# Loads of v on SyncE's queue instead of ScalarE's, and a last tile in two halves: windowed attention and an MLP mixer on one Trainium2 core

## The chip, the cores and the metric

The kernel runs on one core of a Trainium2 chip. The metric is the device time of one execution in microseconds: the median of the runs shown. The profile is one further execution, recorded by the hardware profiler; its times count from the span's start, the first instruction.

## The reference

Eight batches, eight heads, 576 positions, head size 64. Attention is allowed within 32 positions, and to and from 8 global positions given in `global_idx`. A token mixer and a channel mixer follow, each with a residual.

```python
scores = scale * np.matmul(q, k.transpose(0, 1, 3, 2))      # mask: |i-j| <= 32, or i or j global
attn = softmax(np.where(mask, scores, -1e9))
x = np.matmul(attn, v).transpose(0, 2, 1, 3).reshape(8, 576, 512)
h = np.maximum(x.transpose(0, 2, 1) @ w_tok1, 0) @ w_tok2   # 576 -> 256 -> 576
u = x + h.transpose(0, 2, 1)
out = u + np.maximum(u @ w_ch1, 0) @ w_ch2                  # 512 -> 1536 -> 512
```

Inputs and output are float32; the kernel computes in float16 with float32 sums.

## The kernel before, in words

Each batch goes through the same steps, and two batches are in flight.

- **Loads** (`loads`, L922): q and k in two pieces of four heads (`lq`, `lk`, L504), their last 64 rows (`lr`, L514), and v in five row chunks (`lv`, L523). Each of these tiles exists once, so a load of the next batch waits for the casts of this one. Batches 0 to 2 are loaded by SP and POOL; batches 3 to 7 have q and k on SP's queue and v on ACT's (L946).
- **Casts** to float16: `qk` (L534), `rn` (L531), `vsh` (L546). `vod` is `vsh` moved by 64 rows (L554).
- **Transposes** of q and k: by PE for batches 0 to 2, by DMA transposes on SP's queue for batches 3 to 7 (`rawr` L639, `raw` L643: one and eight for a batch), which DVE copies into `qT` and `kT` (L646 to L654).
- **Scores and values**: PE's scores (L673), ACT's exponential `e` (L683), DVE's mask (L689) and a copy for the global sums (`eg`, L692); global queries and keys in `lf`, `rf`; values (L740, L753), divided by DVE into `x` (L781).
- **Token mixer**: L803, relu `a` L812, L821, and `u` = x + h (L834; the last 64 rows of two batches share one tile `ul`, L837). `u` is transposed into `uT` by PE (L848, L850) or DMA (L853), `ul` into `uTl` (L843).
- **Channel mixer**: 12 groups of L866 (`chan1`) with relu `b` (L858 on ACT or L860 on DVE), L878 for the tile of `ul` (`b1l`), then L895 (`chan2`) for four row tiles of a batch and, once for two batches, the last tile of `ul`. DVE adds `u` to the bank and writes `osb` (L903, three buffers in turn), which is stored (L906 by POOL, by SP in the last batch; L909 for the last tile, 64 rows to each batch).

Nothing of the order is written out. Each step is recorded with `op`: its engine choices with an estimated cost, a priority, what it reads and writes, the PSUM bank it needs, and for a DMA an estimated work, packet count and delay. `run` (L119) is a list scheduler that runs while the program is built: it picks, engine by engine, what could start first by those estimates, and so fixes each engine's order and which of the eight PSUM banks a matmul group uses. On the chip each engine runs its list strictly in that order, and waits at a step whose input isn't there. So a changed estimate for a DMA moves compute on other engines.

The calls of the loads of batches 3 to 7, with the estimated issue times in the brackets, in us:

```python
            load_rest(b, pl, [("S", 0.65)])
            ...
                    load_qk(b, ti, slice(h, h + 4), pl + 1 + h / 2, [("S", 0.5)])
            load_v(b, pl + 6, [("A", 0.6)])
```

Of the kernel before, what the change touches and what calls it, by code (L numbers as in the profile page):

```python
# [8 lines left out]
F32 = mybir.dt.float32  # L9
# [6 lines left out]
P = 128  # L16
# [11 lines left out]
def kernel(  # L28
# [12 lines left out]
    nc = tc.nc  # L41
    B, H, S, D = q.shape
# [5 lines left out]
    NJ = DCH // P  # L48
    assert S == 576 and D == 64 and DM == 512 and DTOK == 256 and DCH == 1536
    LAST = S - P * (NT - 1)  # L50
# [27 lines left out]
    uls = [const.tile([P, DM], F16, name=f"ul{i}") for i in range(2)]  # L78
# [3 lines left out]
    b1l = const.tile([P, NJ, P], F16, name="b1l")  # L82
    osbs = [const.tile([P, DM], F32, name=f"osb{i}") for i in range(3)]
# [35 lines left out]
    def run(free, look, hop, warm_until):  # L119
# [41 lines left out]
        def drain(t):  # L161
            if t > clock[0]:
                flow(rings, clock[0], t)
                clock[0] = t
# [28 lines left out]
        while ready:  # L193
            cand = {}
            for i in ready:
                o = ops[i]
                t0, sl = 0.0, None
                if o["new"]:
                    sl = slot(o["new"][0], len(o["new"][1]), max([free["P"]] + list(at[i].values())))
                    if sl is None:  # L200
                        continue
                    t0 = max(t0, max(x[0] for x in sl))
                best = None
                for k, (e, c) in enumerate(o["opts"]):
                    st = max([free[e], t0] + [f + (hop if x != e else 0.0) for x, f in at[i].items()])
                    if o["dma"]:
                        ln, z = lanes["G" if e == "G" else "S"], filled["A" if e == "K" else e]
                        if len(ln) >= 8:
                            st = max(st, max(ln[-8], ln[-7], ln[-6]) + 2.5 if e == "A" else ln[-8])
                        room, x = RING - o["dma"][3], len(z)  # L210
                        while x and room >= z[x - 1][1]:
                            room -= z[x - 1][1]
                            x -= 1
                        if x:
                            st = max(st, z[x - 1][0])
                    if e == "P" and o["mode"] != mode:
                        c = c + 0.095
                    key = (st + c + 0.25 * k, e, st, c)
                    if best is None or key < best:
                        best = key  # L220
                cand.setdefault(best[1], []).append((best[2], o["pri"], i, best[3], sl))
            assert cand, ("stuck", banks, [(ops[i]["opts"], ops[i]["pri"], ops[i]["new"] and ops[i]["new"][1]) for i in ready])
            pick = None
            for e, cs in cand.items():
                lim = min(x[0] for x in cs) + look[e]
                x = min((x for x in cs if x[0] <= lim), key=lambda x: (x[1], x[0], x[2]))
                if pick is None or x[0] < pick[1][0]:
                    pick = (e, x)
            e, (st, _, i, c, sl) = pick
            o = ops[i]  # L230
            if e == "P":
                gap, spare = st - free["P"], [k for k in range(8) if (banks[k][1] is None or not open_uses[banks[k][1]]) and banks[k][0] <= free["P"]]
                if st < warm_until and gap > 0.52 and spare:
                    warm(min(spare, key=lambda k: (banks[k][0], k)), int((gap - 0.3) / (0.22 if st < 12.0 else 0.12)))
                mode = o["mode"]
            if o["new"]:
                kind, keys, shape, dt = o["new"]
                for key, (_, k) in zip(keys, sl):
                    home[key] = [k, k + 1] if kind == "S" else [k]
                    for z in home[key]:  # L240
                        banks[z] = (0.0, key)
                    ps_tile[key] = view(k, shape, dt)
            o["fn"](e)
            free[e] = st + c
            f = st + c + LAT[e]
            if o["dma"]:
                work, size, lag, packets = o["dma"]
                q = "A" if e == "K" else e
                drain(min(f, min(free[x] for x in "GSA")))
                f = land(q, f, work, size, i)  # L250
                filled[q].append((f, packets))
                f += lag
                lanes["G" if e == "G" else "S"].append(f)
                f += o["late"] + (LATE if st > 36.0 else 0.3)
            fin[i] = f
            log.append((st, f, e, i, max(o["deps"], key=lambda x: fin[x]) if o["deps"] else None))
            ready.discard(i)
            for key in o["ps"]:
                open_uses[key] -= 1
                for z in home[key]:  # L260
                    banks[z] = (max(banks[z][0], f + hop), key)
            for u in users[i]:
                left[u] -= 1
                if i in ops[u]["behind"]:
                    at[u][e] = max(at[u].get(e, 0.0), st + c)
                else:
                    x = "D" if o["dma"] else e
                    at[u][x] = max(at[u].get(x, 0.0), f)
                if not left[u]:
                    ready.add(u)  # L270
# [614 lines left out]
    nout = [0]  # L885

    def chan2(b, tau, pri):
        i, key = b % 2, ("o", b, tau)
        last = tau == NT - 1
        js = [range(0, 4), range(4, 8), range(8, 12)] if b == 0 else [range(0, 6), range(6, 12)]  # L890
        for part, jr in enumerate(js):
            def f(e, jr=jr):
                for j in jr:
                    w = b1l[:, j, :] if last else b1[:, j, P * tau : P * tau + P]
                    nc.tensor.matmul(ps_tile[key], lhsT=w, rhs=wc2[:, j, :], start=(j == 0), stop=(j == NJ - 1))  # L895
            r = [("wc2", t) for t in sorted({j // 4 for j in jr})]
            r += [("b1l", t) for t in range(3)] if last else [("b1", j) for j in range(NJ)]
            op([("P", 0.2165 * len(jr))], pri - 0.5 * part if b else pri + 5 * part, f, r=r, ps=[key], new=("M", [key], [P, 512], F32) if part == 0 else None)
        o = nout[0] % 3
        nout[0] += 1  # L900
        osb = osbs[o]
        def g(e):
            nc.vector.tensor_add(out=osb, in0=uls[b // 2 % 2] if last else u16s[i][:, tau], in1=ps_tile[key])  # L903
        op([("V", 0.62)], pri - 8, g, r=[("ul", b // 2 % 2, 0), ("ul", b // 2 % 2, 1)] if last else [("u", i, tau)], ps=[key], w=[("osb", o)])
        if not last:
            op([("G", 0.56) if b < B - 1 else ("S", 0.45)], pri + 5, lambda e: ENG[e].dma_start(out=out[b, P * tau : P * tau + P, :], in_=osb), r=[("osb", o)], dma=STORE)  # L906
        else:
            for z in range(2):
                op([("S", 0.45)], pri + 5, lambda e, z=z: nc.sync.dma_start(  # L909
                    out=out[b - 1 + z, S - LAST : S, :], in_=osb[64 * z : 64 * z + 64]), r=[("osb", o)], dma=(0.39, 2048, 0.8, 64))  # L910
# [11 lines left out]
    def loads(b, n0=0):  # L922
        pl = 100.0 * b - 145 if b != 1 else -174.0
        if b == 0:
            load_rest(0, -196, [("S", 0.65)])
            for hs in (slice(0, 2), slice(2, 4), slice(4, 8)):
                for ti in range(2):
                    load_qk(0, ti, hs, -195 + hs.start, [("S", 0.6)])
            load_v(0, -180, [("S", 0.6)])
            gate(-178, [("lv", NT - 4)], [lv[:, NT - 4, 0, 0:1]])  # L930
            return
        if b < PEB:
            if b == 1:
                pl = -173.9
            load_rest(b, pl, [("G", 0.73)], [n0] if b == 1 else ())
            for h in range(0, H, 4):
                for ti in range(2):
                    load_qk(b, ti, slice(h, h + 4), pl + 1 + h / 2 if b > 1 else pl + 0.1 + h / 100, [("G", 0.88)], [n0] if b == 1 else ())
            if b > 1:
                load_v(b, pl + 6, [("G", 0.87)])  # L940
        else:
            load_rest(b, pl, [("S", 0.65)])
            for h in range(0, H, 4):
                for ti in range(2):
                    load_qk(b, ti, slice(h, h + 4), pl + 1 + h / 2, [("S", 0.5)])
            load_v(b, pl + 6, [("A", 0.6)])  # L946

    def casts(b):
        pc = 100.0 * b - 140
# [109 lines left out]
```

## Time and profile before

| what | value |
|---|---|
| median of 3 runs | 314.24 us (314.05 to 315.2) |
| the profiled execution's own time | 314.6 us |
| its span, first to last instruction | 312.9 us, 7276 instructions |
| TensorE clock granted, mean | 0.987 |
| HBM read, written | 36.11 MB, 9.44 MB |
| transfers: SP's queue (q1), POOL's (q0), ACT's (q10) | 26.49, 18.45, 5.90 MB |

How to read it: PE is the matmul engine, PEld its weight loads, DVE VectorE, ACT ScalarE, POOL GpSimd, SP SyncE, which only issues transfers; SPq and ACTq rows are issues by those engines. A row of a timeline gives start and duration in us, engine, line, operation, output and inputs with shapes, and in brackets how long the engine was idle just before and what ended that. Lines such as L903 are those of the kernel before.

### The profile page before, as it was taken

How to read it: one execution, taken by the hardware profiler on the slowest of the kernel's cores; microseconds unless marked ns; L12 is line 12 of the kernel's file. 1: busy time of each engine (PE TensorE's matmuls, PEld its weight loads, DVE VectorE, ACT ScalarE, POOL GpSimd, SP SyncE). 2: the span in 40 equal slices, each digit the busy share in tenths (PEclk: the TensorE clock that was granted, in tenths of full speed). 3: DMA queues.
4: the chain of work that ended last, by engine and by line, in shares of the span. 5: the costliest groups of instructions: out<-in, count | busy, mean ns of one | idle time of the engine just before them, and what ended most of it. 6: DMA issues, size and time to landing. Idle time of an engine off the chain costs nothing.

```text
span 312.9 us, 7276 instructions
## 1 busy us (share of the span) xinstructions
PE 292.0 (93%) x2943; PEld 154.4 (49%) x2943; DVE 186.8 (60%) x410; ACT 180.5 (58%) x325; POOL 60.5 (19%) x109
## 2 busy tenths in 40 slices
PE   6979889997999979988999998999999999999994
PEld 4755545454474434533456444544555445444641
DVE  7789667569686674876675846964543357230021
ACT  4864895377987758841989376733742083305500
POOL 8589635632001100002000110002000200020000
PEclk9989999999999979999999999999999999999998
DMA  6989999999999999999979999924003211051013
GB/s 183 255 129 287 208 222 222 287 243 234 214 212 220 194 267 318 118 190 221 325 114 176 203 313 189 159 50 136 36 0 63 89 53 37 12 140 69 2 67 102
DMA packets 94660, 51.31 MB, mean 164 GB/s; under 512 B 73698, under 2 KB 89954, under 8 KB 94626
## 3 DMA queue, kind: packets, MB, share of 16 engines
q1 hardware_dynamic: 62480, 26.49, 40.3%
q0 software_dynamic: 8704, 18.45, 24.0%
q10 hardware_dynamic: 23442, 5.90, 11.1%
q8 instruction: 23, 0.38, 0.5%
q14 instruction: 11, 0.09, 0.1%
HBM read 36.11 MB, written 9.44 MB: 146 GB/s over the span
## 4 chain that ended last, share of the span: by engine, by line
PE 58%; DMA 26%; ACT 5%; DVE 5%; issue 2%; SPq 2%; POOL 1%; POOLq 0%; ACTq 0%; DVEq 0%
PE bank L895 22%; PE bank L866 21%; DMA lv<-in_v_dram 8%; DMA raw<-qk 6%; DMA lq<-in_q_dram 5%; PE bank L821 4%; DMA g_q<-in_q_dram,idx_i 3%; PE bank L673 3%; PE bank L803 2%; DMA lk<-in_k_dram 2%; PE bank L878 2%; ACT qk L534 2%; ACT vsh L546 2%; DVE osb L903 2%; PE bank L753 1%
## 5 line engine op out<-in xcount | busy, mean ns | idle before, releaser
L866 PE MATMUL bank<-uT,wc 128*128 128x512 f16 x384 | 94.0, 384 | 6.4 <-DVE osb L903 2.3
L895 PE MATMUL bank<-wc,b 128*128 128x512 f16 x384 | 88.3, 379 | 2.9 <-DVE osb L903 2.2
L858 ACT ACTIVATE b<-bank 128x512 f16<-128x512 f32 x88 | 52.5, 617 | 38.3 <-PE bank L866 38.3
L683 ACT ACTIVATE e<-bank 128x648 f16<-128x648 f32 x64 | 42.7, 737 | 30.0 <-PE bank L673 29.8
L895 PEld LDWEIGHTS <-b 128*128 128x128 f16 x384 | 36.7, 98 | 45.9 <-issue 4.2
L866 PEld LDWEIGHTS <-wc 128*128 128x128 f16 x384 | 35.2, 98 | 48.5 <-issue 8.7
L906 POOL DMA_DIRECT2D out_dram<-osb x28 | 16.1, 574 | 203.1 <-DVE osb L903 203.0
L903 DVE TENSOR_TENSOR osb<-u,bank 128x512 f32<-128x512 f16 x32 | 21.9, 686 | 45.3 <-PE bank L895 41.5
L546 ACT CAST vsh<-lv 128x512 f16<-128x512 f32 (+3 forms) x44 | 26.5, 620 | 9.7 <-DMA uT<-u 5.3
L689 DVE TENSOR_TENSOR e<-e,masku 128x1296 f16<-128x1296 f16 x28 | 23.3, 831 | 13.7 <-ACT e L683 13.2
L834 DVE TENSOR_TENSOR u<-x,bank 128x512 f16<-128x512 f16 x30 | 18.7, 681 | 15.0 <-PE bank L821 14.8
L781 DVE TENSOR_TENSOR x<-bank,rr 128x512 f16<-128x512 f32 x32 | 22.1, 691 | 1.1
L821 PE MATMUL bank<-a,w 128*128 128x512 f16 x80 | 20.1, 379 | 0.5 <-DVE a L809 0.3
L534 ACT CAST qk<-lq 128x512 f16<-128x512 f32 x26 | 16.2, 626 | 4.5 <-DMA lq<-in_q_dram 2.0
L803 PE MATMUL bank<-x,w 128*128 128x512 f16 x64 | 18.7, 379 | 0.0
L673 PEld LDWEIGHTS <-kT 64*128 64x128 f16 x576 | 11.2, 97 | 14.4 <-issue 13.6
L534 ACT CAST qk<-lk 128x512 f16<-128x512 f32 x27 | 16.9, 631 | 1.8 <-DMA lk<-in_k_dram 1.8
L654 DVE COPY qT<-raw 128x512 f16<-128x512 f16 x20 | 12.0, 602 | 7.2 <-DMA raw<-qk 7.1
L753 PEld LDWEIGHTS <-e 128*64 128x64 f16 x576 | 16.1, 116 | 0.1
L740 PE MATMUL bank<-rf,lf 128*64 128x264 f16 x144 | 15.6, 293 | 0.5 <-DVE rf L726 0.5
L753 PE MATMUL bank<-vsh,e 128*64 128x66 f16 x320 | 16.0, 199 | 0.0
L673 PE MATMUL bank<-qT,kT 64*128 64x72 f16 x576 | 15.4, 198 | 0.0
(164 smaller groups left out, 333.6 us busy)
## 6 DMA issues: line engine op xcount, KB each, us to landing
out_dram<-osb POOLq DMA_DIRECT2D x28, 256.0 KB, 4.3
lq<-in_q_dram SPq DMA_DIRECT2D x11, 512.0 KB, 6.4
lk<-in_k_dram SPq DMA_DIRECT2D x11, 512.0 KB, 7.9
lv<-in_v_dram ACTq DMA_DIRECT2D x15, 256.0 KB, 4.6
wc<-in_moe_w_ch_dram POOLq DMA_DIRECT2D x6, 512.0 KB, 12.8
lq<-in_q_dram POOLq DMA_DIRECT2D x4, 512.0 KB, 6.4
lk<-in_k_dram POOLq DMA_DIRECT2D x4, 512.0 KB, 11.0
lv<-in_v_dram ACTq DMA_DIRECT2D x10, 192.0 KB, 3.8
```

Of the source, the lines that this page charges most:

```text
L534: COPY[e](out=qk[:, ti, p].rearrange("q i (r d) -> q r i d", r=2), in_=(lq, lk)[ti][:, hs])
L546: COPY[e](out=vsh[i][a:z, c, :, 0:D], in_=lv[a:z, c])
L673: nc.tensor.matmul(ps_tile[keys[z]][:, u // 3, UW * (u % 3) : UW * (u % 3) + UW], lhsT=kT[r, 64 * u : 64 * u + P], rhs=qT[r, u // 2, UW * ...
L683: op([("A", 0.595)], pri + 1, lambda e, par=par: nc.scalar.activation(out=es[i][:, 2 * p + par].rearrange("p (n u) x -> p n u x", n=3), in ...
L689: op([("V", 0.85)], pri + 2, lambda e: nc.vector.tensor_mul(out=e2, in0=e2, in1=masku.unsqueeze(1).to_broadcast([P, 2, NB, UW])), r=["mask ...
L753: nc.tensor.matmul(o[:, VW * hh : VW * hh + VW], lhsT=es[i][:, h, 2 * tau + c, x : x + 64], rhs=vod[i][:, tau, h, :] if c else vsh[i][:, t ...
L803: nc.tensor.matmul(ps_tile[key][:, tt], lhsT=w, rhs=x16s[i][:, ch, :], start=(ch == 0), stop=(ch == NT - 1))
L821: nc.tensor.matmul(ps_tile[key], lhsT=w2[:, ch, P * tau - sh : P * tau - sh + P], rhs=a1[:, ch, :], start=(ch == 0), stop=(ch == 1 and not ...
L858: nc.scalar.activation(out=out, in_=in_, func=AF.Relu)
L866: nc.tensor.matmul(ps_tile[key], lhsT=wc1[:, cc, P * j : P * j + P], rhs=uT[:, cc, :], start=(cc == 0), stop=(cc == 3))
L895: nc.tensor.matmul(ps_tile[key], lhsT=w, rhs=wc2[:, j, :], start=(j == 0), stop=(j == NJ - 1))
L903: nc.vector.tensor_add(out=osb, in0=uls[b // 2 % 2] if last else u16s[i][:, tau], in1=ps_tile[key])
```

## The change

Three edits. The v loads of batches 3 to 7 are issued by SP, with an estimated 1.0 us each, and the estimate for an issue of a q or k load of these batches goes from 0.5 to 1.15 us. The scheduler also holds SP back when ACT issues a transfer, by 0.9 us per 1024 packets; with v gone from ACT, only the new stores at the end are such transfers. And the last tile of the last batch (64 rows each of batches 6 and 7) is computed as two halves of 256 columns, each with its own bank and its own addition, and each stored by two transfers, one on SP's queue and one on ACT's. Since the estimates changed, the scheduler orders SP, ACT, DVE and PE anew from batch 3's loads on. POOL's order is the same.

```diff
             if o["dma"]:
                 work, size, lag, packets = o["dma"]
                 q = "A" if e == "K" else e
+                if e == "A":
+                    free["S"] = max(free["S"], st) + 0.9 * o["dma"][3] / 1024
                 drain(min(f, min(free[x] for x in "GSA")))
...
     def chan2(b, tau, pri):
         i, key = b % 2, ("o", b, tau)
         last = tau == NT - 1
+        if last and b == B - 1:
+            osb = osbs[nout[0] % 3]
+            for z in range(2):
+                cs, kz = slice(256 * z, 256 * z + 256), ("o", b, tau, z)
+                def f(e, cs=cs, kz=kz):
+                    for j in range(NJ):
+                        nc.tensor.matmul(ps_tile[kz], lhsT=b1l[:, j, :], rhs=wc2[:, j, cs], start=(j == 0), stop=(j == NJ - 1))
+                op([("P", 1.31)], pri + z, f, r=[("wc2", t) for t in range(3)] + [("b1l", t) for t in range(3)], ps=[kz], new=("M", [kz], [P, 256], F32))
+                op([("V", 0.4)], pri - 8, lambda e, cs=cs, kz=kz: nc.vector.tensor_add(out=osb[:, cs], in0=uls[b // 2 % 2][:, cs], in1=ps_tile[kz]),
+                   r=[("ul", b // 2 % 2, 0), ("ul", b // 2 % 2, 1)] + ([] if z else [("osb", nout[0] % 3)]), ps=[kz], w=[("osbz", z)])
+                for y in range(2):
+                    op([("SA"[y], 0.45)], pri + 5 + z, lambda e, y=y, cs=cs: ENG[e].dma_start(
+                        out=out[b - 1 + y, S - LAST : S, cs], in_=osb[64 * y : 64 * y + 64, cs]), r=[("osbz", z)], dma=(0.25, 1024, 0.8, 64))
+            return
...
-                    load_qk(b, ti, slice(h, h + 4), pl + 1 + h / 2, [("S", 0.5)])
-            load_v(b, pl + 6, [("A", 0.6)])
+                    load_qk(b, ti, slice(h, h + 4), pl + 1 + h / 2, [("S", 1.15)])
+            load_v(b, pl + 6, [("S", 1.0)])
```

SP's order around the loads of batch 4 shows the move: `raw` and `rawr` are the transposes of batch 3, then of batch 4. Before:

```order
L643 DMA_TRANSPOSE raw<-qk 128x4x128 x3
L504 DMA lq<-in_q_dram 128x4x256
L504 DMA lk<-in_k_dram 128x4x256
L643 DMA_TRANSPOSE raw<-qk 128x4x128 x4
L504 DMA lq<-in_q_dram 128x4x256
L504 DMA lk<-in_k_dram 128x4x256
L639 DMA_TRANSPOSE rawr<-rn 128x4x128
L643 DMA_TRANSPOSE raw<-qk 128x4x128 x8
```

And now (line numbers of the changed kernel are 2 higher here, and 16 higher from its new stores on):

```order
L506 DMA lq<-in_q_dram 128x4x256
L645 DMA_TRANSPOSE raw<-qk 128x4x128 x5
L506 DMA lk<-in_k_dram 128x4x256
L506 DMA lq<-in_q_dram 128x4x256
L506 DMA lk<-in_k_dram 128x4x256
L525 DMA lv<-in_v_dram 96x8x64
L525 DMA lv<-in_v_dram 128x8x64 x3
L525 DMA lv<-in_v_dram 96x8x64
L641 DMA_TRANSPOSE rawr<-rn 128x4x128
L645 DMA_TRANSPOSE raw<-qk 128x4x128 x8
```

All five v loads of batch 4 now stand between its q and k loads and its transposes.

## The prediction

> **What bounds the kernel now.** I read the page first: busy time and the chain of waits.
>
> ```profile
> PE 292.0 (93%) x2943; PEld 154.4 (49%) x2943; DVE 186.8 (60%) x410; ACT 180.5 (58%) x325; POOL 60.5 (19%) x109
> PE 58%; DMA 26%; ACT 5%; DVE 5%; issue 2%; SPq 2%; POOL 1%; POOLq 0%; ACTq 0%; DVEq 0%
> ```
>
> PE is busy 292.0 of 312.9 us; a quarter of the chain is DMA, though, so some of PE's idle time is decided by landings. The tile view of lv shows where the moved loads are (ns min/median/max, first and last start):
>
> ```profile
> L523 ACTq DMA_DIRECT2D lv<-in_v_dram x25: 337/391/1265, 69.2 to 199.4; - x25
> ```
>
> Nothing moves before 69 us, so I cut the span from 60 on into stretches: us of PE, PEld, DVE, ACT and POOL busy, PE clock, DMA share, GB/s.
>
> ```profile
> 60.00:80.00 20.00, 18.10 (x174) 9.52 (x172) 13.99 (x26) 14.96 (x29) 5.40 (x8) 1.00 1.15 228
> 80.00:100.00 20.00, 19.58 (x250) 11.38 (x243) 14.04 (x31) 18.38 (x34) 0.86 (x1) 1.00 1.11 212
> 100.00:120.00 20.00, 17.79 (x156) 8.05 (x155) 13.67 (x28) 12.24 (x22) 1.77 (x3) 0.91 1.13 255
> 120.00:140.00 20.00, 19.66 (x188) 9.78 (x187) 13.97 (x33) 14.55 (x26) 0.00 (x0) 1.00 1.05 186
> 140.00:160.00 20.00, 18.22 (x199) 8.56 (x198) 12.90 (x24) 12.91 (x25) 2.19 (x4) 1.00 0.90 230
> 160.00:180.00 20.00, 19.57 (x187) 11.09 (x184) 15.71 (x32) 12.36 (x22) 1.39 (x2) 1.00 1.12 188
> 180.00:200.00 20.00, 19.16 (x255) 9.80 (x253) 13.02 (x31) 15.72 (x30) 1.08 (x2) 1.00 1.17 240
> 200.00:310.00 110.00, 108.18 (x903) 54.08 (x901) 44.32 (x82) 40.92 (x70) 6.48 (x12) 1.00 0.21 62
> ```
>
> From 60 to 200 us the DMA engines are full (share 0.90 to 1.17). PE idles 1.90, 0.42, 2.21, 0.34, 1.78, 0.43 and 0.84 us in the seven rows, 7.9 together. In the third it also loses 0.09 of its clock, 20 x 0.09 = 1.8 us. After 200 only the end is idle. So 9.7 us is all that the middle can give. The timelines of PE and DVE say who made the large gaps (in brackets: idle time before, and releaser).
>
> ```profile
> 73.30 1.02 PE L866 MATMUL bank<-uT,wc 128*128 128x512 f16 x4 [1.62 <-DVE qT L589]
> 113.27 1.85 PE L866 MATMUL bank<-uT,wc 128*128 128x512 f16 x4 [2.08 <-DVE osb L903]
> 141.94 5.34 PE L895 MATMUL bank<-wc,b 128*128 128x512 f16 x24 [1.78 <-DVE osb L903]
> 192.48 0.46 PE L720 MATMUL bank<-vsh,eg 128*32 128x132 f16 x17 [0.84 <-DVE eg L692]
> ```
>
> ```profile
> 69.69 0.23 DVE L617 CAST g_q<-g_q 128x128 f16<-128x128 f32 x1 [2.06 <-DMA g_q<-in_q_dram,idx_i]
> 109.65 0.62 DVE L654 COPY qT<-raw 128x512 f16<-128x512 f16 x1 [1.52 <-DMA raw<-qk]
> 112.03 0.59 DVE L654 COPY qT<-raw 128x512 f16<-128x512 f16 x1 [1.25 <-DMA raw<-qk]
> 112.54 0.68 DVE L903 TENSOR_TENSOR osb<-u,bank 128x512 f32<-128x512 f16 x1
> 134.75 0.61 DVE L654 COPY qT<-raw 128x512 f16<-128x512 f16 x1 [2.50 <-DMA raw<-qk]
> 190.33 0.23 DVE L646 COPY qT<-rawr 128x256 f16<-128x256 f16 x1 [2.03 <-DMA rawr<-rn]
> ```
>
> The same story three times: DVE runs in order, reaches a copy of a DMA transpose that hasn't landed, and the addition behind it (osb, or the mask of e and its eg) is late, so PE finds no free bank or no input. At 73.30 it is a gather instead, issued before anything changes: 1.9 us that stay.
>
> **The change, part by part.** *The v loads.* 25 issues leave ACT for SP.
>
> ```profile
> q10 hardware_dynamic: 23442, 5.90, 11.1%
> DMA to landing us min/median/max: 2.5/4.8/8.5
> 98.45 1.19 SPq L639 DMA_TRANSPOSE rawr<-rn  x1
> 99.75 12.26 SPq L643 DMA_TRANSPOSE raw<-qk  x8
> 112.07 0.62 SPq L514 DMA_DIRECT2D lr<-in_q_dram  x1
> 115.47 0.93 SPq L504 DMA_DIRECT2D lk<-in_k_dram  x1
> 122.81 1.20 SPq L909 DMA_DIRECT2D out_dram<-osb  x2
> 147.96 0.54 SPq L504 DMA_DIRECT2D lk<-in_k_dram  x1
> 158.25 1.22 SPq L639 DMA_TRANSPOSE rawr<-rn  x1
> ```
>
> ACT wins 25 x 0.39 = 10 us in which it could not run, but it is 58% busy and only one small PE gap (0.43) names it: at most 0.4. SP pays at least 25 x 0.62 = 16 us of issues. Its idle time hides them (it issues nothing from 116.4 to 122.8 or from 148.5 to 158.2); what counts is who stands behind. ACT's queue (q10) was busy 0.111 x 312.9 = 34.7 us, 1.39 us of all engines per load. Five loads ahead of a batch's nine transposes put up to 5 x 1.39 = 6.9 us before them in one queue, against landings of 4.8 us now (raw, third row). Against that, v of the batch before no longer runs beside the transposes, since it landed earlier, and the bytes are the same.
>
> By the Trainium skill, "DMA: Bandwidth & Descriptors", section "Issuing engines are not separate DMA queues", transfers of all issuing engines run on the same 16 engines and a second issuer saves only the sequencer's time. By that rule alone the move would be worth nothing on PE; the full DMA share agrees, and it speaks against any gain in bandwidth.
>
> *The order.* So the gain, if any, is that the scheduler, told of dearer SP issues, puts the dependent copies elsewhere. DVE before the 2.08 us gap, and now (osb_102 to 104 are osb0 to 2; the third osb row is the one PE waited for):
>
> ```order
> L646 COPY qT_72<-rawr 128x4x64
> L648 COPY kT_74<-rawr 128x4x64
> L903 TENSOR_TENSOR osb_104<-u_1_95,bank 128x512
> L654 COPY qT_72<-raw 128x4x128
> L903 TENSOR_TENSOR osb_102<-u_1_95,bank 128x512
> L651 COPY kT_74<-raw 128x512
> L654 COPY qT_72<-raw 128x4x128
> L651 COPY kT_74<-raw 128x512
> L654 COPY qT_72<-raw 128x4x128
> L903 TENSOR_TENSOR osb_103<-u_1_95,bank 128x512
> ```
>
> ```order
> L919 TENSOR_TENSOR osb_104<-u_1_95,bank 128x512
> L648 COPY qT_72<-rawr 128x4x64
> L650 COPY kT_74<-rawr 128x4x64
> L556 COPY vod_78<-vsh_76 64x2112
> L919 TENSOR_TENSOR osb_102<-u_1_95,bank 128x512
> L653 COPY kT_74<-raw 128x512
> L919 TENSOR_TENSOR osb_103<-u_1_95,bank 128x512
> ```
>
> Five raw copies stood ahead of osb_103, now one. That takes 4 x 0.6 = 2.4 us of work and the waits of 1.52 and 1.25 off its path and adds one vod copy. So the gap closes unless the transposes land over 4 us later. They may: bounds are 0 and -2.2 of idle, -1.8 of clock. I take half the idle and the whole clock loss, since a gap of 1.78 us cost no clock at 141.94: **-2.9**. At 134.75 five raw copies ahead of the u additions become two: bounds 0 and -2.1 (1.78 + 0.34), I take **-1.2**. At 190.33 all transposes of batch 7 go behind the values of batch 5: **-0.8** (0 to -0.84). The 0.42 and 0.43: **-0.4** (0 to -0.85).
>
> *New waits.* ACT before the exps of batch 3's scores, before and now (vsh_76 is v of batch 4):
>
> ```order
> L850 COPY uT<-bank 128x4x128
> L534 CAST qk<-lq 128x2x4x64
> L534 CAST qk<-lk 128x2x4x64
> L523 DMA lv<-in_v_dram 128x8x64
> L683 ACTIVATE e_81<-bank 128x648 x4
> ```
>
> ```order
> L548 CAST vsh_76<-lv 32x8x64
> L548 CAST vsh_76<-lv 64x8x64
> L852 COPY uT<-bank 128x4x128
> L548 CAST vsh_76<-lv 128x8x64 x3
> L548 CAST vsh_76<-lv 96x8x64
> L685 ACTIVATE e_81<-bank 128x648 x2
> ```
>
> All six v casts now stand ahead of exps that PE needs. They came later before; the third row below is the first of them, the first row batch 3's last q/k cast:
>
> ```profile
> 91.16 0.61 ACT L534 CAST qk<-lk 128x512 f16<-128x512 f32 x1
> 108.09 1.31 ACT L683 ACTIVATE e<-bank 128x648 f16<-128x648 f32 x2 [1.65 <-PE bank L673]
> 121.42 1.89 ACT L546 CAST vsh<-lv 32x512 f16<-32x512 f32 x3
> ```
>
> The loads follow three q/k loads on SP. Counting from about 92, when that cast frees lk: an estimated 3 x 2 us (512 KB at 250 GB/s), 6.9 for v and 2 to land give 107, against the exps at 108.09. It fits by 1 us. On DVE one more raw copy of batch 3 goes ahead of batch 2's rf, which PE awaits: 0 up to the 1.52 of a raw wait, I take half, 0.7. For the casts, 0 up to the 4 us of the slower rival below; a third, 1.3. Together **+2.0** (0 to +5.5).
>
> *The last tile.* 12 matmuls of 512 columns become 24 of 256, two additions, four stores.
>
> ```profile
> 292.38 2.85 PE L878 MATMUL bank<-uTl,wc 128*128 128x128 f16 x48
> 305.43 2.75 PE L895 MATMUL bank<-wc,b1l 128*128 128x512 f16 x12
> 308.22 0.69 DVE L903 TENSOR_TENSOR osb<-ul,bank 128x512 f32<-128x512 f16 x1 [1.90 <-PE bank L895]
> 308.93 1.12 SPq L909 DMA_DIRECT2D out_dram<-osb  x2
> out_dram<-osb SPq DMA_DIRECT2D x2, 128.0 KB, 2.3
> ```
>
> A weight load with its matmul runs in 59 ns (2.85 / 48), below the 108 ns of 256 columns, so the 12 more cost 0 (at most 12 x 0.059 = 0.7). The last addition is half as wide: between 0.35 and 0.69, I take 0.45, -0.24. Its two stores leave on two queues at once instead of 0.56 apart: -0.56. They carry 64 KB each; no row shows that size, so between 0 and half of 2.3, I take 0.2. The first half's pair is issued about 1.3 us earlier, behind PE. Sum **-1.0** (-1.9 to +0.7). ACT has no work left there and issues freely.
>
> The Trainium skill's "DMA: Bandwidth & Descriptors", section "Rules for kernel authors", says of two transfers to disjoint partition halves "Don't bother", as they share the engines. By that rule only the 0.56 and the addition would be left, -0.8; no run here shows it yet.
>
> **Sum**: -1.0 - 2.9 - 1.2 - 0.8 - 0.4 + 2.0 = -4.3 from the profiled execution's 314.6 gives 310.3. That execution stands 0.36 above the median of 314.24, so **309.9**.
>
> **Rivals.** The landing of a q/k load, from the page, serves for the second:
>
> ```profile
> lk<-in_k_dram SPq DMA_DIRECT2D x11, 512.0 KB, 7.9
> ```
>
> *Only the tail* (the waits move but stay): 314.24 - 1.0 = 313.2. For it: the DMA share is full either way, and the gaps follow the landings. Against it: DVE's order puts fewer copies ahead. *Slower*: v lands late and ACT's exps of batch 3 wait behind the casts. It decides once the last v load lands after 108. With lk landing 7.9 after an issue at about 97 (as the q/k loads of batch 4 went before the 98.45 row) and 6.9 of v behind it, 112 is possible: 4 us of new PE idle, and all old gaps stay: 314.24 - 1.0 + 4 = 317.2. For it: nine transposes now share one queue with v. Against: SP can issue v earlier than ACT did, as it does not wait for ACT's work. *All gaps close* but the first, no new waits: 314.24 - 1.0 - 7.75 = 305.5, where 7.75 is 9.65 less 1.9.
>
> **Chances**: forecast 0.5, only the tail 0.2, slower 0.17, all gaps 0.13. A measurement here tells 0.5% (1.6 us) from no change. The forecast's own range is 308 to 312; the range over the cases is 306.0 to 315.0. Faster by over 0.5% (below 312.7): 0.5 + 0.13 and a little of the tail case, 0.64; same 0.19; slower 0.17.
>
> **What would show it.** Right: PE idle from 60 to 200 us near 4.5 instead of 7.9, clock 1.00 from 100 to 120, no DVE wait on raw ahead of an osb that PE waits for, and the end about 3.7 us after the last matmul instead of 4.7 (312.9 less 308.2). Wrong: ACT waiting on DMA lv ahead of the exps at 108, DVE waiting on raw longer than 2.5 us, or landings of raw well over 4.8.

## The result, and the profile after

The change makes the kernel slower: 323.62 us (median, 322.01 to 324.74) against 314.24, a ratio of 1.0288 with a 95% interval of 1.0229 to 1.0348. The forecast was 309.9. The profiled execution has a span of 320.3 us (before 312.9).

The page of the changed kernel, busy time and chain:

```profile
PE 292.2 (91%) x2955; PEld 154.6 (48%) x2955; DVE 186.5 (58%) x410; ACT 180.2 (56%) x326; POOL 60.6 (19%) x109
PE 47%; DMA 17%; ACT 15%; DVE 9%; SPq 6%; issue 4%; POOL 0%; ACTq 0%
```

PE does the same work (292.0 before). All that was lost is idle time. SP's own issues (SPq) are 6% of the chain, 2% before, and ACT 15% where it had 5%. Busy time by stretch, with the columns of the prediction (PE, PEld, DVE, ACT, POOL, PE clock, DMA share, GB/s):

```profile
60.00:80.00 20.00, 18.29 (x175) 9.53 (x174) 14.90 (x27) 16.07 (x31) 5.28 (x7) 1.00 1.09 260
80.00:100.00 20.00, 17.66 (x229) 10.34 (x227) 14.00 (x30) 16.00 (x30) 0.00 (x0) 1.00 1.11 173
100.00:120.00 20.00, 16.87 (x158) 8.05 (x158) 12.34 (x24) 15.40 (x28) 2.47 (x4) 1.00 1.03 209
120.00:140.00 20.00, 18.25 (x192) 9.37 (x185) 13.64 (x33) 14.24 (x25) 0.00 (x0) 1.00 0.88 223
140.00:160.00 20.00, 19.59 (x183) 8.82 (x183) 13.62 (x26) 11.27 (x22) 2.47 (x4) 1.00 0.83 216
160.00:180.00 20.00, 16.06 (x188) 9.56 (x183) 11.88 (x25) 11.49 (x21) 0.00 (x0) 1.00 0.83 147
180.00:200.00 20.00, 19.83 (x238) 9.87 (x238) 10.94 (x23) 13.54 (x26) 2.98 (x4) 1.00 0.97 248
200.00:220.00 20.00, 16.73 (x114) 7.44 (x109) 14.47 (x29) 7.93 (x14) 0.54 (x1) 0.91 0.52 92
```

PE idles 16.7 us from 60 to 220; before it idled 7.9 from 60 to 200 and nothing from 200 to 220. That is 8.8 us more. The stretch of slow clock (0.91, so 0.09 x 20 = 1.8 us) is still there, now at 200 to 220. The end is 1.0 us shorter, and the first 60 us, which nothing changes, ran some 0.5 us ahead here: 8.8 - 1.0 - 0.5 = 7.3 of the span's 7.4. The DMA share falls to 0.83 to 0.97 after 120, where it was 0.90 to 1.17: the DMA engines stand idle more, not less.

PE's large gaps, from its timeline:

```profile
87.93 0.42 PE L742 MATMUL bank<-rf,lf 128*64 128x264 f16 x4 [1.64 <-DVE rf L728]
113.61 2.13 PE L868 MATMUL bank<-uT,wc 128*128 128x512 f16 x8 [2.49 <-DVE osb L919]
177.19 1.46 PE L911 MATMUL bank<-wc,b 128*128 128x512 f16 x6 [1.77 <-DVE u L836]
180.17 5.34 PE L911 MATMUL bank<-wc,b 128*128 128x512 f16 x24 [1.52 <-DVE osb L919]
215.22 2.72 PE L911 MATMUL bank<-wc,b 128*128 128x512 f16 x6 [2.75 <-DVE u L836]
```

DVE is late each time, 10.2 us of the 16.7 together. Its timeline has what it stood at:

```profile
111.73 0.23 DVE L648 COPY qT<-rawr 128x256 f16<-128x256 f16 x1 [6.07 <-DMA rawr<-rn]
169.79 0.23 DVE L648 COPY qT<-rawr 128x256 f16<-128x256 f16 x1 [4.94 <-DMA rawr<-rn]
175.83 0.59 DVE L653 COPY kT<-raw 128x512 f16<-128x512 f16 x1 [1.86 <-DMA raw<-qk]
208.65 0.61 DVE L653 COPY kT<-raw 128x512 f16<-128x512 f16 x1 [3.14 <-DMA raw<-qk]
```

Behind the first of these waits comes the osb addition that PE misses at 113.61; the next two stand ahead of the u additions that it misses at 177.19, and the last ahead of those at 215.22. ACT makes smaller gaps, 3.8 us together, of which these are the largest:

```profile
100.56 1.47 PE L823 MATMUL bank<-a,w 128*128 128x512 f16 x6 [1.21 <-ACT qk L536]
136.99 2.32 PE L823 MATMUL bank<-a,w 128*128 128x512 f16 x10 [1.19 <-ACT a L814]
```

Before, the first of DVE's waits was 1.31 us:

```profile
105.19 0.23 DVE L646 COPY qT<-rawr 128x256 f16<-128x256 f16 x1 [1.31 <-DMA rawr<-rn]
```

So batch 4's `rawr` is there 6.5 us later (111.73 less 105.19). SP's timeline shows where these microseconds went:

```profile
96.80 0.51 SPq L506 DMA_DIRECT2D lk<-in_k_dram  x1
97.40 7.75 SPq L525 DMA_DIRECT2D lv<-in_v_dram  x5
105.27 1.32 SPq L641 DMA_TRANSPOSE rawr<-rn  x1
107.14 11.12 SPq L645 DMA_TRANSPOSE raw<-qk  x8
187.51 10.31 SPq L525 DMA_DIRECT2D lv<-in_v_dram  x5
```

Five v loads hold SP for 7.75 us, 1.55 each, and for batch 7 for 2.06 each. An issue that had 0.62 us in the prediction and 1.0 in the scheduler takes 1.25 us in the median (the tile view of lv), and `rawr` stands behind five of them. Once issued, a transpose now lands sooner than before, in 2.7 us instead of 4.8 (the tile view of raw):

```profile
L525 SPq DMA_DIRECT2D lv<-in_v_dram x25: 449/1253/3502, 68.5 to 195.9; - x25
DMA to landing us min/median/max: 2.4/2.7/5.7
```

The transposes wait ahead of their issue, not in the queue. The end of the program went as forecast:

```profile
313.84 2.78 PE L898 MATMUL bank<-wc,b1l 128*128 128x256 f16 x24
315.80 1.78 SPq L903 DMA_DIRECT2D out_dram<-osb  x2
316.66 0.42 DVE L900 TENSOR_TENSOR osb<-ul,bank 128x256 f32<-128x256 f16 x1 [0.89 <-PE bank L898]
```

24 matmuls take 2.78 us where 12 took 2.75, and the end comes 3.7 us after the last of them (320.3 less 316.62) instead of 4.7.

### The profile page after: what moved, and what is told of

The parts are those of the page before. It is cut to its first block, busy times and chain, and to the rows that moved or that the text cites. A ratio compares the mean times of both kernels' runs of the same rounds, so it can differ in the third digit from the quotient of the medians.

```text
span 320.3 us, 7348 instructions
## 1 busy us (share of the span) xinstructions
PE 292.2 (91%) x2955; PEld 154.6 (48%) x2955; DVE 186.5 (58%) x410; ACT 180.2 (56%) x326; POOL 60.6 (19%) x109
## 4 chain that ended last, share of the span: by engine, by line
PE 47%; DMA 17%; ACT 15%; DVE 9%; SPq 6%; issue 4%; POOL 0%; ACTq 0%
PE bank L911 19%; PE bank L868 14%; DMA lk<-in_k_dram 8%; ACT e L685 5%; DMA raw<-qk 3%; ACT b L860 3%; DMA lv<-in_v_dram 3%; PE bank L823 3%; PE bank L880 3%; DMA g_k<-in_k_dram,idx_i 2%; PE bank L805 2%; SPq L525 2%; DVE u L836 2%; ACT qk L536 2%; PE bank L675 2%
## 5 line engine op out<-in xcount | busy, mean ns | idle before, releaser
L911 PE MATMUL bank<-wc,b 128*128 128x512 f16 x384 | 89.7, 383 | 7.8 <-DVE u L836 4.5
L868 PE MATMUL bank<-uT,wc 128*128 128x512 f16 x384 | 92.6, 380 | 4.5 <-DVE osb L919 2.5
L922 POOL DMA_DIRECT2D out_dram<-osb x28 | 16.7, 596 | 211.6 <-DVE osb L919 211.6
L836 DVE TENSOR_TENSOR u<-x,bank 128x512 f16<-128x512 f16 x30 | 18.7, 682 | 12.6 <-PE bank L823 12.4
L675 PEld LDWEIGHTS <-kT 64*128 64x128 f16 x576 | 11.1, 96 | 14.5 <-issue 14.5
L653 DVE COPY kT<-raw 128x512 f16<-128x512 f16 x20 | 12.0, 598 | 9.5 <-DMA raw<-qk 9.4
```

Source lines behind the costliest of these rows:

```text
L675: nc.tensor.matmul(ps_tile[keys[z]][:, u // 3, UW * (u % 3) : UW * (u % 3) + UW], lhsT=kT[r, 64 * u : 64 * u + P], rhs=qT[r, u // 2, UW * ...
L836: nc.vector.tensor_add(out=u16s[i][:, tau], in0=x16s[i][:, tau], in1=ps_tile[key])
L868: nc.tensor.matmul(ps_tile[key], lhsT=wc1[:, cc, P * j : P * j + P], rhs=uT[:, cc, :], start=(cc == 0), stop=(cc == 3))
```

## The experiments

Theory A: v loads on SP stand ahead of the transposes and hold SP, so that transposes (and later q/k loads) go out late. Rival B: the new estimates gave a bad order, whatever the queue. Rival C: not SP, but the bytes of v ahead of the transposes on full DMA engines. Single runs of the kernel before spread from 310.8 to 317.9 us over these experiments (median 314.05 to 314.36), so differences under 1.5 us are read from the intervals only.

**The last tile alone.** The block `if last and b == B - 1` of the change, in the kernel before.

> Only the last tile in two halves with its four stores; all loads as before. The trace of the changed kernel has 3.7 us from the last matmul to the end, before had 4.7. If the tail gain is independent of the rest: 1.0 us faster, ratio 0.997, and everything ahead of the last tile as before. If the halves cost PE time (24 weight loads), 0 to 0.7 of it is lost.

312.99 us, ratio 0.9978 (0.9935 to 1.0021). The run times can't tell 1.0 us from nothing; the trace can: its last matmul ends at 306.52 and its span at 310.2, again 3.7 us. The tail gains 1.0 us and is innocent.

**The move alone**, with the old estimates:

```diff
-            load_v(b, pl + 6, [("A", 0.6)])
+            load_v(b, pl + 6, [("S", 0.6)])
```

> v of batches 3 to 7 issued by SP, with issue estimates of 0.6 us for v and 0.5 for q and k as before; last tile as before. Theory A (each v issue holds SP 1.55 to 2.06 us and so the transposes behind it go late): slower at least as much as the changed kernel, 324.6 us or more, as the scheduler now expects the transposes even earlier; DVE waits on rawr and raw over 20 us in all. Rival B (the raised estimates gave a bad order): near 314, with rawr waits near the 4.3 us of before.

328.71 us, ratio 1.0463 (1.0397 to 1.0530): 14.5 us slower, 5.1 above the changed kernel (1.0 of that is the tail). DVE's waits on raw and rawr sum to 21.5 us (before 12.6, changed kernel 23.9). B falls as the cause: with v on SP, the raised estimates make the time about 4 us better, not worse.

**The estimate alone**, v on ACT:

```diff
-                    load_qk(b, ti, slice(h, h + 4), pl + 1 + h / 2, [("S", 0.5)])
+                    load_qk(b, ti, slice(h, h + 4), pl + 1 + h / 2, [("S", 1.15)])
```

> v stays on ACT's queue; only the estimate for a q or k issue of batches 3 to 7 goes from 0.5 to 1.15 us. Rival B (estimates, and the order that follows from them, cost the time): 319 us or more. Theory A (SP held by v): within 2 us of 314.2, and SP still gets from the q/k loads to rawr within 1.5 us.

313.69 us, ratio 0.9997 (0.9954 to 1.0040). No difference; B is out.

**Half of v.** The changed kernel, with every engine's order as it is, but four of the eight heads of v are not loaded for batches 3 to 7:

```diff
-                    out=lv[r0:r1, c], in_=v[b, :, j0 : j0 + (r1 - r0), :].rearrange("h p d -> p h d")
+                    out=lv[r0:r1, c, 0:n], in_=v[b, 0:n, j0 : j0 + (r1 - r0), :].rearrange("h p d -> p h d")   # n = 4 if b >= PEB else H
```

> The changed kernel, order the same on every engine, but the v loads of batches 3 to 7 fetch four of the eight heads (the other half of v is left out, stale values are used). Theory A: an SP issue of v falls from 1.6 to at most 0.9 us, rawr goes out 3 to 4 us earlier, the DVE waits on rawr fall from 12.7 to under 6 us, and the time falls by 4 to 8 us to 316 to 319. Rival B (the order itself): the same order gives the same gaps, within 1.5 us of 323.6.

311.41 us, ratio 0.9921 (0.9880 to 0.9961): 12.2 below the changed kernel, more than the 4 to 8 expected, with the same order. SP's timeline of this run:

```profile
95.67 5.19 SPq L526 DMA_DIRECT2D lv<-in_v_dram  x5
100.97 1.25 SPq L642 DMA_TRANSPOSE rawr<-rn  x1
```

Five issues take 5.19 us instead of 7.75, `rawr` goes out 4.3 us earlier, and DVE's waits on rawr fall from 12.7 to 5.2 us. The order of the changed kernel is good; the amount of v ahead of the transposes spoils it. (It also moves fewer bytes, so it can't tell A from C.) A load of half the size is also a smaller instruction, so this run doesn't say why an issue got shorter. In the changed kernel, loads of 192 and 256 KB took 0.45, 1.41, 2.70 and 1.17 us, the first four of the run of five at 97.40: the length is not the instruction's own. That SP waits for room behind what it issued before is likely, and not shown.

**v issued by ACT at the same places.** The changed kernel, modelled as before, the instruction sent to ACT:

```diff
-                ENG[e].dma_start(
+                (nc.scalar if b >= PEB else ENG[e]).dma_start(
```

> The changed kernel with its order and its bytes, except that the 25 v loads are issued by ACT, at the place in the program where SP had them. The half-v run cut bytes and issue time together; this one keeps the bytes. Theory A (SP held by v issues, transposes behind it late): rawr goes out 5 us or more earlier after the last q/k load, DVE waits on rawr under 6 us, time 311 to 316. Theory C (the bytes of v ahead of the transposes on the full DMA engines): transposes still land late, DVE waits on rawr 10 us or more, time over 319.

335.63 us, ratio 1.0694 (1.0602 to 1.0785): against both expectations. DVE's waits on rawr are down to 0.9 us, as A wanted, but now ACT is held. Its timeline:

```profile
77.30 5.20 ACTq L525 DMA_DIRECT2D lv<-in_v_dram  x1
82.60 0.60 ACT L860 ACTIVATE b<-bank 128x512 f16<-128x512 f32 x1 [4.92 <-issue]
117.03 0.34 ACTq L525 DMA_DIRECT2D lv<-in_v_dram  x1
117.41 0.62 ACT L536 CAST qk<-lq 128x512 f16<-128x512 f32 x1 [7.38 <-DMA raw<-qk]
```

One v issue takes 5.20 us. The wait of 7.38 us in the last row lies ahead of the v issue at 117.03: ACT stood there until one of SP's transposes had landed. Here v held ACT as it had held SP. The run separates A from C no further.

**Transposes taken to land 6 us later** by the scheduler, in the changed kernel:

```diff
-                    r=[("qk", ti, p)], w=[("raw", ti, p)], dma=TURN)
+                    r=[("qk", ti, p)], w=[("raw", ti, p)], dma=TURN, late=6.0)
```

(the same for `rawr`).

> The changed kernel, but the scheduler takes every DMA transpose of q and k to land 6 us later, so it puts DVE's copies of them further back; loads and queues as in the changed kernel. If DVE's waits on rawr and raw, ahead of osb, u and rf, carry the loss to PE: DVE waits on them fall from 24 us to under 10 and the time to 313 to 317. If PE is late because the scores themselves lack q and k: no gain, 322 or more.

320.43 us, ratio 1.0228 (1.0167 to 1.0289). DVE waits on raw and rawr no more at all, yet only 3.2 us come back. ACT's and PE's timelines show the second path:

```profile
101.66 1.14 ACT L536 CAST qk<-lk 128x512 f16<-128x512 f32 x2 [3.46 <-DMA lk<-in_k_dram]
125.66 0.62 ACT L533 CAST rn<-lr 128x512 f16<-128x512 f32 x1 [4.83 <-DMA lr<-in_k_dram]
```

```profile
129.98 0.43 PE L742 MATMUL bank<-rf,lf 128*64 128x264 f16 x2 [2.00 <-ACT b L860]
```

The q/k loads of the next batch go out late too: the first lk for batch 4 at 97.04, behind five transposes (88.69 in the kernel before), and the first lr for batch 5 at 121.28, behind v and batch 4's nine transposes (112.07 before). ACT waits for them at its casts, with relus that PE needs behind. The DVE path, which I had as the whole loss, is part of it. How much the copies cost by being moved back themselves, this run doesn't say.

**The estimates set to what was measured**: 1.8 us for v, 0.6 for q/k.

```diff
-                    load_qk(b, ti, slice(h, h + 4), pl + 1 + h / 2, [("S", 1.15)])
-            load_v(b, pl + 6, [("S", 1.0)])
+                    load_qk(b, ti, slice(h, h + 4), pl + 1 + h / 2, [("S", 0.6)])
+            load_v(b, pl + 6, [("S", 1.8)])
```

> The changed kernel with the estimate of a v issue on SP at 1.8 us (measured: 1.55 to 2.06 for five in a row) and of a q/k issue at 0.6 (measured 0.5 to 0.6). If the loss is what the estimates still miss of SP's time: better than the changed kernel by 3 to 7 us, 317 to 320. If v on SP costs whatever the order: 322 or more.

317.18 us, ratio 1.0136 (1.0071 to 1.0201): 6.4 us better than the changed kernel, as expected, and still slower than before. An honest price takes off about half of the loss by the ratios (1.4% against 2.9%), two thirds by the medians; it can't move v, whose priority stands ahead of the transposes.

**v on POOL's queue**, in the changed kernel:

```diff
-            load_v(b, pl + 6, [("S", 1.0)])
+            load_v(b, pl + 6, [("G", 0.87)])
```

> The changed kernel with v of batches 3 to 7 issued by POOL (estimate 0.87 us). Takes v out of SP's and ACT's way. Theory A: SP is free as before, rawr waits near 4 us, 311 to 315. Against it: v then shares POOL's queue with the output stores, which wait for osb; if a v load stands behind a store that waits, ACT's v casts are late and the time is 318 or more.

329.91 us, ratio 1.0517 (1.0441 to 1.0594). SP is free, but the tile view of rawr says that it now lands late:

```profile
L641 SPq DMA_TRANSPOSE rawr<-rn x5: 1512/2319/4222, 79.2 to 181.0; - x5
DMA to landing us min/median/max: 2.6/10.2/15.9
```

10.2 us in the median (4.3 in the changed kernel, 6.0 before). From 99 to 118 us, with batch 4's `rawr` under way for 15.9 us, POOL's queue took 59.8% of the DMA engines' time. This fits C: bytes beside a transpose delay it from another queue too. The stores that I named as the danger cost something as well: at 78.68 an osb addition has waited 2.03 us for a store, and PE idles 1.97 us behind it.

**v behind the transposes.** Changed kernel, same queue and estimates; each batch's v loads may go only after its last transpose has been issued:

```diff
-            load_v(b, pl + 6, [("S", 1.0)])
...
             turn_dma(b, ca - 38)
+            load_v(b, ca - 34, [("S", 1.0)], [n for n in range(len(ops)) if ops[n]["dma"] is TURN][-1:])
```

(the casts of v are recorded after it).

> The changed kernel, v still on SP's queue with the same estimates, but each batch's five v loads are held back until its nine transposes have been issued. Theory A/C (what costs is v standing ahead of the transposes): rawr goes out within 1 us of the last q/k load as before, DVE waits on rawr and raw fall to about 12 us (before: 11.7), time 311 to 316. If v on SP's queue costs wherever it stands: 320 or more.

309.47 us, ratio 0.9825 (0.9776 to 0.9873): 14.2 us below the changed kernel and faster than the kernel before. SP's timeline of this run:

```profile
98.10 0.73 SPq L506 DMA_DIRECT2D lk<-in_k_dram  x1
98.94 2.51 SPq L641 DMA_TRANSPOSE rawr<-rn  x1
101.56 12.29 SPq L645 DMA_TRANSPOSE raw<-qk  x8
113.90 4.08 SPq L525 DMA_DIRECT2D lv<-in_v_dram  x5
```

`rawr` follows lk at once, and five v issues hold SP only 4.08 us, with no transposes waiting behind them. DVE's waits on raw and rawr are 11.3 us (12.6 before), PE idles 5.8 us from 60 to 200. v on SP's queue is no cost; its place was. (ACT's v casts move back with the loads, and the order of the other engines with them.)

**The same with estimates of 0.6** for q, k and v:

> As the run with v behind the transposes, with issue estimates of 0.6 us for q, k and v instead of 1.15 and 1.0. If only the place of v matters: the same within 2 us. If the raised estimates carry the recovery: 3 us or more slower than it.

314.29 us, ratio 0.9966 (0.9907 to 1.0024): some 5 us above the run before it, so the raised estimates are worth as much here as with v in front. They count once v is on SP. Nearly the same low estimates with v in front of the transposes or among them, in the move alone, gave 328.71, of which 1.0 is the tail: the place of v is worth some 13 us here, 14 with the raised ones.

**SP held without bytes.** The kernel before, with five tiny transfers ahead of each `rawr`:

```diff
+            for s in spare:   # five tiles of 1 x 16
+                nc.sync.dma_start(out=s, in_=bass.AP(tensor=gt32, offset=0, ap=[[0, 1], [1, 2 * NG]]))
             nc.sync.dma_start_transpose(out=rawr, in_=rn.rearrange("p n x -> p (n x)"))
```

> The kernel before, with v on ACT, and five transfers of 64 bytes issued by SP ahead of each batch's rawr for batches 3 to 7, unknown to the scheduler: they hold SP without bytes on the DMA engines. Theory A (SP being held is the cost): rawr goes out 3 us or more later, time 3 to 7 us above 314. Theory C (v's bytes ahead of the transposes are): under 1.5 us.

325.97 us, ratio 1.0351 (1.0278 to 1.0425): 11.6 us, above A's 3 to 7, and far from C's. But it isn't clean: the timelines of ACT and PE show one wait that neither theory had.

```profile
78.50 0.40 ACTq L523 DMA_DIRECT2D lv<-in_v_dram  x1
78.94 2.05 ACT L574 COPY kT<-bank 128x512 f16<-128x512 f16 x4 [7.66 <-DMA lk<-in_k_dram]
```

```profile
80.30 0.22 PE L678 MATMUL bank<-qT,kT 64*128 64x72 f16 x1 [6.80 <-DVE qT L569]
```

ACT stood 7.66 us at its own v issue until one of SP's loads had landed, and PE lost 6.8. The scheduler's rule (L207 to L209) has SP's and ACT's transfers share eight lanes, a transfer waiting for the eighth before it; five more transfers put ACT's issue behind another one. That this is the reason was not tried. The small transfers held SP for 1.5 to 4.5 us a batch, less than v's five loads (7.75 at batch 4). From 80 to 220 us PE idles 10.7 us (6.0 before), but not for SP alone: ACT still waits there at v issues for transposes (0.99 us up to 143.23, with a gap of 1.78 us for PE behind it). So 4.7 us is the most that holding SP cost in that stretch, and this run doesn't prove A.

**Estimate and last tile, without the move:**

> The kernel before with two parts of the change: the estimate of 1.15 us for q and k issues, and the last tile in halves; v stays on ACT's queue. From the two alone (ratios 0.9997 and 0.9978): 312.5 to 313.5, the best of the kernels with v on ACT.

313.23 us, ratio 0.9955 (0.9915 to 0.9994), as expected: the tail's 1.0 us and no more.

Together: v ahead of the transposes is what costs the time (v behind, with either set of estimates, and half of v show it). In the changed kernel it makes the transposes late by holding SP, as its timeline shows; from POOL's queue they were late with SP free, most likely by v's bytes. How much of the changed kernel's loss is SP's issue and how much the engines' backlog stays open: if SP is slow to issue because the backlog hasn't drained, the two are one wait.

## Why the prediction was wrong

- **What bounds the kernel** was right: PE, with 9.7 us of idle time and slow clock between 60 and 200 us, mostly DVE standing at a copy of a transpose. The same mechanism made most of the loss.
- **"SP pays at least 25 x 0.62 = 16 us of issues. Its idle time hides them"** is the step that failed. The eight v groups in SP's timeline sum to 39 us. 0.62 was the row of a single lr load, of another shape. The row for five v loads in a run was in the trace of before, on SP, and I passed it by:

```profile
5.57 9.06 SPq L523 DMA_DIRECT2D lv<-in_v_dram  x5
```

  1.8 us each, within the 1.55 to 2.06 that the change then showed for five in a run. And SP's idle time did not hide them: they stand where `rawr` should have gone out.
- **"Up to 5 x 1.39 = 6.9 us before them"** had the right size (6.5 measured) with the wrong place: it is spent ahead of the issue, not in the queue. Whether the sizes agree by more than luck stays open.
- **"The gap closes unless the transposes land over 4 us later"** was right as a condition, and 6.9 stood beside it. I then took half the idle and all the clock loss as gain, -2.9, against my own bound. Measured: the gap of 2.08 is one of 2.49. It cost no clock this time; a loss of the same size (1.8) stands at 200 to 220, around another gap. It is true that one raw copy instead of five stands ahead of osb; it doesn't help when `rawr`, also ahead of it, is 6 us late.
- **-1.2 and -0.8**: the two gaps did close (0.41 us idle from 140 to 160, 0.17 from 180 to 200), but others of 1.77, 1.52 and 2.75 opened, where a late rawr or raw stands ahead of u, and u ahead of osb. I followed the copies that moved back and didn't ask which now stood in front.
- **New waits, +2.0**: the rf term was 1.64 instead of 0.7. The v casts ahead of the exps cost ACT 0.97 us at `DMA lv`. No PE gap names them, but in the gap of 1.19 us at 136.99 ACT's `a` comes right after v casts. The slower rival (317.2) had the right sign, and the shared queue among its reasons, but put the wait on ACT's exps; it came by DVE's copies and, for less, ACT's q/k casts.
- **The range.** 306.0 to 315.0 leaves out the prediction's own rivals at 305.5 and 317.2. Its terms at their worst give 314.24 + 0.7 + 5.5 = 320.4, still short of 323.62: no term let an old gap grow or a new one open on DVE behind a late transpose, beyond the 1.5 us at rf.
- **The last tile, -1.0**: right, 4.7 to 3.7 us after the last matmul.
- **The Trainium skill's rule** ("DMA: Bandwidth & Descriptors", section "Issuing engines are not separate DMA queues") agreed in bandwidth: up to 200 us the DMA share rose in no stretch. What I made of it, that SP's time for the issues is small, didn't hold: 39 us.

## What to carry to other kernels

Price an issue from rows of the same load, issued in a run as it will be, not from a single issue of another load. In a queue that issues in order, bulk loads without hurry go behind the small transfers that engines wait for: the same queue, bytes and estimates gave 323.6 us with v in front and 309.5 with v behind. And when copies move in an engine's order, look at which one now stands first.

## What was not expected of the hardware

- The duration of an issue is not fixed by its instruction: over these runs five v issues in a run took SP 3.89 to 10.31 us. Bytes alone don't set it either: four q/k loads of 512 KB in a row went out in 0.51 to 0.62 us each (changed kernel, 119.68 to 121.96), while five v loads of half that size or less took 1.55 each. v moves in smaller pieces (5.90 MB in 23442 packets, 252 bytes each); whether that is the reason was not tried.
- An issue can hold the engine that computes: one v issue held ACT for 5.20 us, and ACT waited 7.38 and 7.66 us at an issue for transfers of SP (why, was not tried).
- A DMA transpose on SP's queue (`raw`) landed 2.7 us (median) after its issue with v ahead of it on the same queue, 4.8 with v on ACT's (3.6 in the run with the changed kernel's order), and 6.1 with v on POOL's.
